# Loads, buffers and softmax steps of the first batch in an attention and two-layer MLP kernel

## The chip, the cores and the metric

The kernel runs on one core of a Trainium2 chip. The metric is the device time of one execution in microseconds (us), taken as the median over repeated runs.

## The reference

Inputs are float32 arrays; the host only rearranges them. Cut to what matters, with `S` = 576 positions, 4 batches, 8 heads of 64:

```python
scores = 0.125 * q @ k.T                              # per batch and head
# heads 0-3 see the last 32 positions, heads 4-7 every fourth of the last 128
scores = np.where(mask, scores, -1e9)
attn = np.exp(scores - scores.max(-1, keepdims=True))
attn = attn / (attn.sum(-1, keepdims=True) + 1e-9)
x = heads_side_by_side(attn @ v)                      # 2304 tokens x 512
x = ((x @ w1) * (x @ w2)) @ w3 @ w_out                # 512 -> 1024 -> 1024 -> 512
g = x @ w_gate
return (g / (1 + np.exp(-g)) * (x @ w_val)) @ w_out2  # 512 -> 1536 -> 512
```

## The kernel before

**Data.** The weights arrive as 8-byte floats in blocks of 1 MB (128 partitions x 2048 words of 32 bits). A block goes into one of four raw buffers (`raw0`, `raw1` and the two halves of `early`) and is converted there by five steps: ScalarE takes up the high words (`conv` piece 0), VectorE shifts the low words (piece 1) and joins both (piece 2), ScalarE rounds to the high part (piece 3), and VectorE subtracts to get the low part (piece 4). Piece 4 writes the weight slot and frees the raw buffer. A product of two float32 matrices is then three matmuls, high by high, high by low and low by high (`mm3`, lines 193 to 195). Every operand, attention's results too, is split into such parts by one ScalarE copy and one VectorE subtraction.

**Work.** Attention runs over 16 pairs of heads, four pairs for each batch. For a pair, TensorE makes the scores of all nine 64-row blocks (line 290), VectorE scales them and adds the mask (`masked`, line 301), takes the row maxima (`maxima`, line 313), ScalarE makes one exponential for each block column, with the row sum beside it (`exps`, line 318), VectorE inverts the sums (`inverse`, lines 323 and 324), and VectorE (first batch) or GpSimd (the others) multiplies (`normed`, line 329). A pair's nine columns are handled in two halves, of four (`g` = 0) and five columns (`g` = 1). Then come three groups of transposes (line 337), their copies (line 341), the products with v (line 355), and `attended`, which splits the result into the parts of x (lines 579 and 582).

The five chunks of tokens go through gates: `gate` k multiplies x by block k of w1 and of w2 (12 matmuls of 512 columns each), multiplies both and splits the product into `p`. `w_steps` multiply w3 by w_out, 512 columns of w3 in part 0 and 512 in part 1, and give the blocks `W`; `contraction` multiplies p by W. The first four gates of chunk 0 stand among the w_steps, since both need only weights, x and one another's buffers.

**Order.** Everything up to chunk 2 is a list of nodes. A node names its engine, an assumed duration, what it comes after and a key; `run_nodes` plays the list through with these assumptions (DMA at `DMA_RATE` MB per us behind one queue) and writes each engine's instructions in the order of that play. On the chip every engine keeps this order and waits by semaphores. So an instruction whose input is late holds up all that stand behind it on its engine. All loads are issued by SyncE (SP) in one such order, and one that has to wait for a buffer holds up those behind. `FIRST`, `EACH`, `START` and `W_AT` are times, in the same play, from which keys are made: the first pair, the distance of the pairs, the first gate and the first two w_steps. Later chunks and the second MLP are written out by hand in program order.

**Before the change** the start of the program loads k and q of pair 0, a mask, the first two weight blocks in four halves, and then k and q of pair 1, and so on; the first two w_steps stand among the attention of pairs 0 to 2. `v` and the scores buffers `s` are two each, used in turn.

Of the kernel before, what the change touches and what calls it, by code (L numbers as in the profile page):

```python
# [24 lines left out]
P = 128  # L25
# [65 lines left out]
FIRST, EACH, START = 4, 6, 36.0  # L91
W_AT = [10, 14]


def moe_chain_kernel(tc, q_in, k_in, v_in, w_in, mask_in, out):
# [8 lines left out]
    with static as st, other as ot, psum as pp, dram as dp:  # L104
# [9 lines left out]
        pr = fp.tile([P, 2, 2, CMAX], F32R, name="p")  # L114
# [99 lines left out]
        def gate_b(name, x, n):  # L214
            project(bb[:, :n], name, x)
            count["p"] += 1
            u, p = ta[:, :n], pr[:, count["p"] % 2, :, :n]
# [28 lines left out]
        att1_pool = tc.tile_pool(name="att1", bufs=1)  # L246
        att2_pool = tc.tile_pool(name="att2", bufs=1, side="right")
        with att1_pool as a1, att2_pool as a2:


            qd = [a1.tile([P, S], F32, name=f"q{i}") for i in range(2)]
            ks = [a1.tile([P, WIN + S], F32, name=f"k{i}") for i in range(2)]
            vv = [a1.tile([P, NBLK, P], F32, name="v0")]
            raw_pool = tc.tile_pool(name="rawx", bufs=1)
            rp = raw_pool.__enter__()
            pr_more = rp.tile([P, 2, 2, CMAX], F32R, name="p2")
            vv.append(rp.tile([P, NBLK, P], F32, name="v1"))
# [7 lines left out]
            sm = [a2.tile([P, 3, NBLK], F32, name=f"sm{i}") for i in range(2)]  # L265
# [7 lines left out]
            def v_of(i):  # L273
                return vv[i % 2 if i < NPAIR else 0]
# [21 lines left out]
            def masked(i, s_mm):  # L296
                s = sc[i % 2]
# [13 lines left out]
            def maxima(i, g):  # L311
                lo, hi = COLS[g]
                nc.vector.tensor_reduce(out=sm[i % 2][:, 0, lo:hi], in_=sc[i % 2][:, lo:hi], op=ALU.max, axis=AX.X, negate=True)  # L313

            def exps(i, g):
                s, m = sc[i % 2], sm[i % 2]
                for n in range(*COLS[g]):
                    nc.scalar.activation(s[:, n], s[:, n], AF.Exp, bias=m[:, 0, n:n + 1], accum_out=m[:, 1, n:n + 1])  # L318

            def inverse(i, g):  # L320
                lo, hi = COLS[g]
                m = sm[i % 2]
# [3 lines left out]
            def normed(i, g):  # L326
                s, m = sc[i % 2], sm[i % 2]
                lo, hi = COLS[g]
                (nc.vector if i < NPAIR else nc.gpsimd).tensor_tensor(
# [4 lines left out]
            def transposes(i, g, got):  # L334
                s = sc[i % 2]
# [319 lines left out]
            def v_loads(i, key=INF, after=()):  # L655
                loads["v", i] = node("SP", 0.47, load_v, i, after=[v_use.get(i - 2 if i <= NPAIR else i - 1), *after], mb=0.44, key=key)

            def attention(i, t, dt, after=()):

                b, hp = divmod(i, NPAIR)  # L660
                s_mm = node("PE", 1.05, scores, i, after=[loads["q", i], *s_use.get(i - 2, []), *after], key=t, take=("bank", 2))
                q_use[i] = s_mm
                m1 = node("DVE", 2 * on_dve(384) + 2 * on_dve(96), masked, i, s_mm, after=[s_mm, *s_use.get(i - 2, [])], give=[(s_mm, None)])
                e, x = [], []
                for g, (lo, hi) in enumerate(COLS):
                    r = node("DVE", on_dve(96 * (hi - lo)), maxima, i, g, after=[m1])
                    ex = node("ACT", (hi - lo) * 0.36, exps, i, g, after=[r])
                    nm = node("DVE", 0.28, inverse, i, g, after=[ex])
                    if i < NPAIR:
# [8 lines left out]
                s_use[i] = ts  # L678
# [3 lines left out]
                for g, cols in enumerate((half_of(i), S - half_of(i))):  # L682
# [4 lines left out]
                    outs.append(node("DVE", on_dve(cols) + 0.1, attended, i, g, 1, v_mm, after=[h, *beyond_use], give=[(v_mm, [g])]))  # L687
# [16 lines left out]
            def p_tile(c, k):  # L704
                return (pr_more[:, k - 2] if c == 0 and 2 <= k < 4 else pr[:, k % 2])[:, :, :CHUNKS[c][1]]

            def gate(c, k, key, dt=2.9):
# [7 lines left out]
                p = p_tile(c, k)  # L715
                buf = k if c == 0 and k < 4 else k % 2
                h, lo = parts(n, ta[:, :n], p[:, 0], p[:, 1], [bo, p_use.get(buf)])
# [35 lines left out]

            def open_stages():
                raw_pool.__exit__(None, None, None)
# [87 lines left out]
            stage_pool = tc.tile_pool(name="stages", bufs=1)  # L843
# [451 lines left out]
```

## Time and profile before

| | |
|---|---|
| median of 3 runs | 842.8 us (841.18, 842.8, 843.55) |
| the profiled execution, its own time | 842.12 us, of which the span of its instructions 839.9 us |
| TensorE (PE) busy | 810.7 us, 97% of the span |
| VectorE (DVE) / ScalarE (ACT) / GpSimd (POOL) busy | 545.5 / 428.8 / 97.0 us |
| mean granted TensorE clock | 0.98 of full speed |
| moved by DMA | 204.18 MB, 243 GB/s over the span |

All times in the rows are from the start of the span. PEld is the loading of stationary operands, which overlaps PE. A row of the timeline gives start, duration, engine, line, operation, tiles and count, and in brackets how long the engine had been idle before it and what ended that. Matmuls overlap, so a row's duration is longer than the distance to the next one. The granted clock has two levels here, 0.5 (1.2 GHz) and 1.0 (2.4 GHz); a value between them is a mean over a stretch.

### The profile page before, as it was taken

The page shows a single profiled execution, that of the slowest core. Times are in us where ns is not written, and L with a number is a line of the kernel's source. Part 1 is how long each engine was busy: PE and PEld are TensorE (multiplying, and loading weights), DVE is VectorE, ACT ScalarE, POOL GpSimd, SP SyncE. Part 2 cuts the span into 40 slices and gives each one's busy share as a digit, 9 for nine tenths or more (in the row PEclk, how much of TensorE's full clock was granted, in tenths as well). Part 3 has the DMA queues.
Part 4 walks back from the last instruction along what each step waited for, and adds up shares of the span by engine and source line. Part 5 has one row for each costly group of instructions (what it writes and reads, how often), then busy time and mean ns, then how long its engine had stood idle before and what let it go on. Part 6 is the DMA issues. An engine that isn't in the chain of part 4 may idle for free.

```text
span 839.9 us, 13927 instructions
## 1 busy us (share of the span) xinstructions
PE 810.7 (97%) x5242; PEld 734.9 (88%) x5242; DVE 545.5 (65%) x976; ACT 428.8 (51%) x1011; POOL 97.0 (12%) x128
## 2 busy tenths in 40 slices
PE   5689999999998999999999999999999999999998
PEld 3578887877786878788899999999999999999997
DVE  5889669486565733475676737587645677564867
ACT  4868387565665643344355634364444354353532
POOL 0000013654554521000000000000000000000000
PEclk7879999999998999999999999999999999999999
DMA  9988254979768850376699877788977787987735
GB/s 263 320 279 291 82 172 160 315 256 314 243 222 300 247 195 22 126 229 229 220 301 392 281 241 265 251 310 268 313 260 257 240 267 249 306 278 239 251 97 175
DMA packets 80530, 204.18 MB, mean 243 GB/s; under 512 B 5840, under 2 KB 41808, under 8 KB 75856
## 3 DMA queue, kind: packets, MB, share of 16 engines
q1 hardware_dynamic: 78736, 200.68, 71.9%
q10 hardware_dynamic: 1728, 2.62, 0.9%
q8 instruction: 41, 0.67, 0.3%
q14 instruction: 25, 0.20, 0.1%
HBM read 160.81 MB, written 42.47 MB: 242 GB/s over the span
## 4 chain that ended last, share of the span: by engine, by line
PE 75%; DMA 9%; DVE 8%; ACT 6%; issue 1%; SPq 1%; POOL 0%; ACTq 0%; DVEq 0%; POOLq 0%
PE bk L193 24%; PE bk L195 23%; PE bk L194 23%; DMA raw<-w_in 7%; ACT s L318 2%; PE bk L355 2%; PE bk L337 1%; DVE raw L820 1%; DVE raw L185 1%; DMA q<-q_in 1%; DVE s L301 1%; ACT raw L181 1%; PE bk L290 1%; ACT stage L831 1%; DVE sm L313 1%
## 5 line engine op out<-in xcount | busy, mean ns | idle before, releaser
L193 PE MATMUL bk<-x,w 128*128 128x512 f32 (+2 forms) x400 | 148.8, 373 | 1.0 <-ACT ta L212 1.0
L195 PE MATMUL bk<-x,w 128*128 128x512 f32 (+2 forms) x400 | 145.8, 365 | 0.0
L194 PE MATMUL bk<-x,w 128*128 128x512 f32 (+2 forms) x400 | 145.8, 364 | 0.0
L193 PEld LDWEIGHTS bk<-x,w 128*128 128x128 f32 x400 | 76.1, 190 | 12.5 <-ACT ta L212 1.6
L195 PEld LDWEIGHTS bk<-x,w 128*128 128x128 f32 x400 | 76.0, 190 | 10.7
L1162 DVE TENSOR_TENSOR acc<-bk,acc 128x384 f32<-128x384 f32 x102 | 56.0, 554 | 44.7 <-PE bk L195 44.5
L194 PEld LDWEIGHTS bk<-x,w 128*128 128x128 f32 x400 | 76.3, 191 | 9.5
L195 PE MATMUL bk<-po,wo 128*128 128x384 f32 x240 | 80.5, 335 | 0.0
L194 PE MATMUL bk<-po,wo 128*128 128x384 f32 x240 | 80.2, 335 | 0.0
L193 PE MATMUL bk<-po,wo 128*128 128x384 f32 x240 | 79.4, 336 | 0.3 <-DVE acc L1162 0.3
L833 POOL TENSOR_TENSOR stage<-raw,stage 128x256 fp32r<-128x256 f32 x96 | 71.4, 777 | 32.3 <-ACT stage L831 32.2
L193 PE MATMUL bk<-w 128*128 128x384 f32 (+1 forms) x216 | 73.1, 341 | 0.0
L194 PE MATMUL bk<-w 128*128 128x384 f32 (+1 forms) x216 | 73.1, 338 | 0.0
L195 PE MATMUL bk<-w 128*128 128x384 f32 (+1 forms) x216 | 72.5, 339 | 0.0
L1087 ACT ACTIVATE u<-bk 128x384 f32<-128x384 f32 x80 | 38.7, 489 | 53.4 <-PE bk L195 53.4
L160 ACT ACTIVATE po<-u 128x768 fp32r<-128x768 f32 (+1 forms) x64 | 50.9, 803 | 26.3 <-PE bk L195 10.5
L161 DVE TENSOR_TENSOR po<-u,po 128x768 fp32r<-128x768 f32 (+1 forms) x64 | 57.4, 902 | 8.7 <-ACT po L160 8.6
L318 ACT ACTIVATE s<-s,sm 128x96 f32<-128x96 f32 x144 | 51.8, 362 | 20.9 <-DVE sm L313 20.9
L195 PE MATMUL bk<-p,W 128*128 128x512 f32 (+1 forms) x160 | 58.3, 369 | 0.0
L194 PE MATMUL bk<-p,W 128*128 128x512 f32 (+1 forms) x160 | 58.2, 368 | 0.0
L193 PE MATMUL bk<-p,W 128*128 128x512 f32 (+1 forms) x160 | 57.7, 380 | 0.0
L181 ACT ACTIVATE raw<-raw 128x1024 f32<-128x1024 f32 (+1 forms) x32 | 34.9, 1090 | 30.0 <-DMA raw<-w_in 30.0
(145 smaller groups left out, 1728.2 us busy)
## 6 DMA issues: line engine op xcount, KB each, us to landing
w<-wd SPq DMA_DIRECT2D x70, 512.0 KB, 4.7
wo<-wod SPq DMA_DIRECT2D x63, 512.0 KB, 4.8
raw<-w_in SPq DMA_DIRECT2D x28, 1024.0 KB, 7.6
mid<-wd SPq DMA_DIRECT2D x42, 512.0 KB, 4.8
wd<-stage SPq DMA_DIRECT2D x16, 896.0 KB, 5.1
early<-w_in SPq DMA_DIRECT2D x8, 1024.0 KB, 7.3
wod<-stage SPq DMA_DIRECT2D x8, 896.0 KB, 6.3
wd<-u SPq DMA_DIRECT2D x8, 896.0 KB, 5.2
```

The lines of the kernel that those rows point to most:

```text
L160: nc.scalar.activation(hi, src, AF.Copy)
L161: return nc.vector.tensor_tensor(out=lo, in0=src, in1=hi.bitcast(F32), op=ALU.subtract)
L181: nc.scalar.activation(hi.bitcast(F32), hi.bitcast(F32), AF.Prelu, scale=REBIAS, alpha=SIGN_UP)
L185: nc.vector.scalar_tensor_tensor(out=lo, in0=hi, scalar=3, in1=lo, op0=ALU.logical_shift_left, op1=ALU.bitwise_or)
L193: nc.tensor.matmul(ps, wh, xh, start=start, stop=False, skip_group_check=onto)
L194: nc.tensor.matmul(ps, wh, xl, start=False, stop=False, skip_group_check=onto)
L195: nc.tensor.matmul(ps, wl, xh, start=False, stop=stop, skip_group_check=onto)
L318: nc.scalar.activation(s[:, n], s[:, n], AF.Exp, bias=m[:, 0, n:n + 1], accum_out=m[:, 1, n:n + 1])
L355: nc.tensor.matmul(banks_of[got[w]][j * D:(j + 1) * D, lo - w * half:hi - w * half], v_of(i)[:KW, n, j * D:(j + 1) * D], pt[:KW, c, z * QB ...
L833: nc.gpsimd.tensor_tensor(out=dst[:, :, 1], in0=src, in1=dst[:, :, 0].bitcast(F32), op=ALU.subtract)
L1087: nc.scalar.activation(t, src, AF.Copy)
L1162: nc.vector.tensor_tensor(out=a, in0=ps, in1=a, op=ALU.add)
```

## The change

The loads of the first batch's q, k, v and masks are keyed in front of all weight blocks, and all weight blocks wait in the plan until the scores of pair 0 are issued. Pairs 0 to 3 get a `v`, an `s` and an `sm` buffer each; these lie in a pool `front`, and the buffers of p, which used to be there from the start, are opened in its place when batch 0 is through with it. Half `g` = 1 of each pair of batch 0 no longer takes five exponentials: GpSimd adds the negated row maxima to the whole half (`shifted`), ScalarE takes one exponential of 480 columns (`exp_all`), and VectorE sums the rows (`sums_of`). The other half keeps its four exponentials. The VectorE node of `attended` gets a key instead of none, for all batches, and the mask is waited for by `masked` instead of by the scores. `parts` inside a gate is written as two nodes (`p_part`), since the p buffers exist only later.

```diff
-FIRST, EACH, START = 4, 6, 36.0
-W_AT = [10, 14]
+FIRST, EACH, START = 4, 5, 36.0
+W_AT = [24, 27]
+WIDE = [(i, 1) for i in range(4)]
+NORMV = [(i, j) for i in range(4) for j in range(2)]
...
-            vv = [a1.tile([P, NBLK, P], F32, name="v0")]
...
+            vv = [a2.tile([P, NBLK, P], F32, name="v0")]
+            front_pool = tc.tile_pool(name="front", bufs=1)
+            fr = front_pool.__enter__()
+            vv += [fr.tile([P, NBLK, P], F32, name=f"v{i}") for i in range(1, NPAIR)]
...
+            sm = [a2.tile([P, 3, NBLK], F32, name=f"sm{i}") for i in range(4)]
+            sc += [fr.tile([P, NBLK, KW], F32, name=f"s{i}") for i in range(2, NPAIR)]
...
+            def shifted(i, g):
+                s, m = sc[sc_of(i)], sm[sc_of(i)]
+                lo, hi = COLS[g]
+                nc.gpsimd.tensor_tensor(
+                    out=s[:, lo:hi], in0=s[:, lo:hi],
+                    in1=m[:, 0, lo:hi].unsqueeze(2).to_broadcast([P, hi - lo, KW]), op=ALU.add,
+                )
+
+            def exp_all(i, g):
+                lo, hi = COLS[g]
+                nc.scalar.activation(sc[sc_of(i)][:, lo:hi], sc[sc_of(i)][:, lo:hi], AF.Exp)
+
+            def sums_of(i, g):
+                lo, hi = COLS[g]
+                nc.vector.tensor_reduce(out=sm[sc_of(i)][:, 1, lo:hi], in_=sc[sc_of(i)][:, lo:hi], op=ALU.add, axis=AX.X)
...
-                    ex = node("ACT", (hi - lo) * 0.36, exps, i, g, after=[r])
+                    if in_one(i, g):
+                        ex = node("POOL", (0.79, 0.95)[g], shifted, i, g, after=[r])
+                        ex = node("ACT", on_act(96 * (hi - lo)), exp_all, i, g, after=[ex])
+                        ex = node("DVE", on_dve(96 * (hi - lo)), sums_of, i, g, after=[ex])
+                    else:
+                        ex = node("ACT", (hi - lo) * 0.36, exps, i, g, after=[r])
...
-                    outs.append(node("DVE", on_dve(cols) + 0.1, attended, i, g, 1, v_mm, after=[h, *beyond_use], give=[(v_mm, [g])]))
+                    outs.append(node("DVE", on_dve(cols) + 0.1, attended, i, g, 1, v_mm, after=[h, *beyond_use], key=t + dt + 5, give=[(v_mm, [g])]))
...
             q_loads(0, 0)
-            mask_at = [node("SP", 0.47, load_mask, slice(0, NHALF), mb=0.2, key=0.1)]
-            for n in range(2):
-                conversion(n, 0.2 + 0.1 * n)
-            q_loads(1, 1)
-            v_loads(0, 2)
-            attention(0, FIRST, 6, mask_at)
...
+            mask_at = [node("SP", 0.47, load_mask, slice(0, NHALF), mb=0.2, key=-9)]
+            q_loads(1, 0.2)
+            v_loads(0, 6)
+            for i in range(NPAIR):
                 if i >= 2:
...
+                    q_loads(i, 0.6)
+                if i == 2:
+                    mask_at.append(node("SP", 0.47, load_mask, slice(NHALF, NHALF + NBLK), after=[q_use[0]], mb=0.44, key=5))
+                if i:
+                    v_loads(i, 6 + i, [q_use[0]])
+                attention(i, FIRST + EACH * i, 6, mask=mask_at[i // 2])
+            for n in range(12):
                 conversion(n, after=[q_use[0]])
...
+            opened = node("SP", 0.0, open_p, after=[*v_use.values(), *[t for ts in s_use.values() for t in ts]])
+            for i in range(NPAIR):
+                p_use[i] = opened
```

**The queue of loads, at the start of the program.** SyncE's rows before; `k0` and `q0` are the buffers of the even pairs, `k1` and `q1` those of the odd ones, and `raw0`, `raw1`, `early` take weights:

```order
L271 DMA k0_101<-k_in 128x576
L268 DMA q0_99<-q_in 128x576
L560 DMA mask_113<-mask_in 128x384
L570 DMA raw0_78<-w_in 128x1024 x2
L570 DMA raw1_79<-w_in 128x1024 x2
L271 DMA k1_102<-k_in 128x576
L268 DMA q1_100<-q_in 128x576
L277 DMA v0_103<-v_in 96x1152
L271 DMA k0_101<-k_in 128x576
L268 DMA q0_99<-q_in 128x576
L560 DMA mask_113<-mask_in 128x864
L277 DMA v1_108<-v_in 96x1152
```

And after the change, from the fifth load on (ahead of these stand a mask, k0, q0 and k1):

```order
L273 DMA q1_96<-q_in 128x576
L282 DMA v0_99<-v_in 96x1152
L276 DMA k0_97<-k_in 128x576
L273 DMA q0_95<-q_in 128x576
L587 DMA mask_110<-mask_in 128x864
L282 DMA v1_103<-v_in 96x1152
L282 DMA v2_104<-v_in 96x1152
L276 DMA k1_98<-k_in 128x576
L273 DMA q1_96<-q_in 128x576
L282 DMA v3_105<-v_in 96x1152
L597 DMA raw0_77<-w_in 128x1024
L597 DMA raw1_78<-w_in 128x1024
```

The first weights stood fourth in the queue; now they stand fifteenth, behind everything that batch 0's attention reads.

**ScalarE at the start of the program.** Before: `raw0`, `raw1` are raw weights, `s0` the scores of pair 0 and `sm0` its maxima and sums, `W2` and `w` weight slots:

```order
L181 ACTIVATE raw0_78<-raw0_78 128x512 x2
L318 ACTIVATE s0_110,sm0_115<-s0_110,sm0_115 128x96 x5
L181 ACTIVATE raw1_79<-raw1_79 128x512
L318 ACTIVATE s0_110,sm0_115<-s0_110,sm0_115 128x96 x4
L174 ACTIVATE W2_74<-raw0_78 128x512
L174 ACTIVATE w_66<-raw1_79 128x512
L181 ACTIVATE raw1_79<-raw1_79 128x512
```

After, with `s1` the scores of pair 1, and `pt` the copies of transposes:

```order
L323 ACTIVATE s0_107,sm0_112<-s0_107,sm0_112 128x96 x4
L341 ACTIVATE s0_107<-s0_107 128x480
L323 ACTIVATE s1_108,sm1_113<-s1_108,sm1_113 128x96 x4
L368 ACTIVATE pt_109<-bk4_85 96x384
L341 ACTIVATE s1_108<-s1_108 128x480
L368 ACTIVATE pt_109<-bk5_86 96x384
```

Five exponentials of 96 columns became one of 480, and no weight stands between the pairs.

**VectorE where pair 12, the first pair of batch 3, is masked.** Before: `raw1` is a weight block of the second MLP, `x0` the parts of x that pair 11's results go to, `s0` with `mask` pair 12:

```order
L582 TENSOR_TENSOR x0_76<-bk7_89,x0_76 128x2x96
L391 COPY beyond_109<-bk7_89 128x2x48
L582 TENSOR_TENSOR x0_76<-bk6_88,x0_76 128x2x96
L391 COPY beyond_109<-bk6_88 128x2x48
L582 TENSOR_TENSOR x1_838<-beyond_109,x1_838 128x2x192 x2
L183 TENSOR_SCALAR raw1_79<-raw1_79 128x1024
L301 SCALAR_TENSOR_TENSOR s0_110<-bk7_89,mask_113 128x384
L301 SCALAR_TENSOR_TENSOR s0_110<-bk7_89,mask_113 64x96
L301 SCALAR_TENSOR_TENSOR s0_110<-bk6_88,mask_113 128x384
L301 SCALAR_TENSOR_TENSOR s0_110<-bk6_88,mask_113 64x96
```

After:

```order
L185 TENSOR_SCALAR raw1_78<-raw1_78 128x1024
L187 SCALAR_TENSOR_TENSOR raw1_78<-raw1_78 128x1024
L609 TENSOR_TENSOR x0_76<-bk7_88,x0_76 128x2x96
L418 COPY beyond_106<-bk7_88 128x2x48
L609 TENSOR_TENSOR x0_76<-bk6_87,x0_76 128x2x96
L418 COPY beyond_106<-bk6_87 128x2x48
L786 COPY o1_80<-bk1_82 128x512
L865 TENSOR_TENSOR raw1_78<-raw1_78 128x256
L609 TENSOR_TENSOR x1_924<-beyond_106,x1_924 128x2x192 x2
L865 TENSOR_TENSOR raw1_78<-raw1_78 128x256 x3
L306 SCALAR_TENSOR_TENSOR s0_107<-bk7_88,mask_110 128x384
L306 SCALAR_TENSOR_TENSOR s0_107<-bk7_88,mask_110 64x96
```

The first VectorE step of the same weight block, which stood right ahead of the masking, now stands ahead of pair 11's results. On TensorE the distance from this pair's scores to its transposes grows from 36 matmuls of 512 columns to 39 and the scores of pair 13.

## Rows read from the trace of the kernel before

**Rows 1.** Windows: busy time by engine, PEclk, DMA share, GB/s.
```profile
0.00:50.60 50.60, 31.25 (x370) 23.06 (x370) 37.26 (x82) 33.40 (x106) 0.82 (x8) 0.75 0.97 294
50.60:78.80 28.20, 28.20 (x123) 23.29 (x122) 26.57 (x32) 21.68 (x24) 0.00 (x0) 0.97 0.79 272
78.80:261.90 183.10, 181.85 (x1361) 145.89 (x1359) 126.52 (x239) 114.63 (x337) 69.83 (x88) 1.00 0.69 232
261.90:264.90 3.00, 0.04 (x1) 0.00 (x0) 2.93 (x8) 2.46 (x10) 1.88 (x3) 0.85 0.90 363
264.90:270.70 5.80, 5.79 (x15) 4.50 (x16) 0.51 (x1) 2.50 (x8) 5.45 (x8) 0.50 0.38 128
270.70:839.90 569.20, 563.54 (x3378) 538.20 (x3376) 351.74 (x617) 254.13 (x530) 19.05 (x22) 1.00 0.72 241
```
**Rows 2.** Timeline of PE: last attention of batch 0, first gate.
```profile
45.53 1.27 PE L337 MATMUL bk<-ident,s 128*96 128x128 f32 x5 [1.34 <-ACT x L579]
48.28 2.40 PE L355 MATMUL bk<-pt,v 96*64 96x64 f32 x40 [1.48 <-ACT pt L341]
50.62 0.80 PE L193 MATMUL bk<-x,w 128*128 128x512 f32 x1
```
**Rows 3.** Timeline of DVE and POOL around pair 12.
```profile
249.68 1.72 DVE L582 TENSOR_TENSOR x<-beyond,x 128x384 fp32r<-128x384 f32 x2
255.52 0.70 DVE L183 TENSOR_SCALAR raw<-raw 128x1024 uint32<-128x1024 uint32 x1 [4.12 <-DMA raw<-w_in]
256.13 1.44 DVE L301 SCALAR_TENSOR_TENSOR s<-bk,mask 128x384 f32<-128x384 f32 x4
...
264.00 0.85 POOL L329 TENSOR_TENSOR s<-s,sm 128x384 f32<-128x384 f32 x1 [0.72 <-DVE sm L324]
```
**Rows 4.** Timeline of PE there: pair 12's scores, a full-clock matmul, the transposes.
```profile
252.50 1.04 PE L290 MATMUL bk<-k,q 64*64 64x96 f32 x36
...
261.55 0.39 PE L195 MATMUL bk<-x,w 128*128 128x512 f32 x1
264.91 0.88 PE L337 MATMUL bk<-ident,s 128*96 128x128 f32 x3 [2.97 <-POOL s L329]
```
**Rows 5.** Issues of loads by SP, and the DMA view's landing of two of them.
```profile
2.12 1.85 SPq L570 DMA_DIRECT2D raw<-w_in  x4
11.12 0.33 SPq L277 DMA_DIRECT2D v<-v_in  x1
38.88 0.33 SPq L570 DMA_DIRECT2D early<-w_in  x1
...
v<-v_in SPq DMA_DIRECT2D x1, 432.0 KB, 11.8
early<-w_in SPq DMA_DIRECT2D x1, 1024.0 KB, 10.2
```
**Rows 6.** Groups of DVE by form, 0 to 100 us: count, busy us, mean ns.
```profile
L185 DVE SCALAR_TENSOR_TENSOR early<-early 128x1024 uint32<-128x1024 uint32 x8 | 9.8, 1222 | 0.2
L183 DVE TENSOR_SCALAR raw<-raw 128x1024 uint32<-128x1024 uint32 x8 | 5.5, 686 | 0.0
L176 DVE TENSOR_TENSOR w<-raw,w 128x1024 fp32r<-128x1024 f32 x4 | 4.9, 1222 | 0.0
L301 DVE SCALAR_TENSOR_TENSOR s<-bk,mask 128x384 f32<-128x384 f32 x8 | 4.4, 548 | 7.3 <-PE bk L290 7.3
L329 DVE TENSOR_TENSOR s<-s,sm 128x480 f32<-128x480 f32 x4 | 2.6, 657 | 0.1
L313 DVE TENSOR_REDUCE sm<-s 128x5 f32<-128x480 f32 x4 | 2.6, 646 | 0.0
```
**Rows 7.** Timeline of DVE: first masking, one block's steps, the last block of part 0.
```profile
7.21 1.45 DVE L301 SCALAR_TENSOR_TENSOR s<-bk,mask 128x384 f32<-128x384 f32 x4 [5.82 <-PE bk L290]
...
60.47 1.23 DVE L176 TENSOR_TENSOR w<-early,w 128x1024 fp32r<-128x1024 f32 x1
61.61 1.22 DVE L185 SCALAR_TENSOR_TENSOR raw<-raw 128x1024 uint32<-128x1024 uint32 x1
62.75 0.69 DVE L582 TENSOR_TENSOR p<-ta,p 128x512 fp32r<-128x512 f32 x1
75.25 1.22 DVE L176 TENSOR_TENSOR W<-early,W 128x1024 fp32r<-128x1024 f32 x1
```
**Rows 8.** Windows for DVE's busy time (third pair of numbers).
```profile
7.20:50.60 43.40, 25.54 (x320) 20.52 (x320) 36.77 (x81) 32.12 (x105) 0.00 (x0) 0.71 1.01 304
0.00:76.50 76.50, 57.15 (x480) 44.46 (x481) 61.53 (x112) 53.56 (x129) 0.82 (x8) 0.82 0.91 288
```
**Rows 9.** Groups: a small exponential on ACT, a multiplication on POOL.
```profile
L318 ACT ACTIVATE s<-s,sm 128x96 f32<-128x96 f32 x36 | 12.9, 361 | 0.5 <-DVE sm L313 0.5
L329 POOL TENSOR_TENSOR s<-s,sm 128x480 f32<-128x480 f32 x12 | 11.9, 993 | 189.8 <-DVE sm L324 167.2 <-ACT s L318 22.6
```
**Rows 10.** Timeline: a VectorE subtraction beside work of POOL.
```profile
202.66 0.86 POOL L329 TENSOR_TENSOR s<-s,sm 128x384 f32<-128x384 f32 x1 [0.72 <-DVE sm L324]
...
202.74 1.32 DVE L582 TENSOR_TENSOR p<-ta,p 128x512 fp32r<-128x512 f32 x1
```

More of the change, by code (lines that the diff above doesn't have):

```diff
@@ L264, in moe_chain_kernel, with sc_of @@
             ident = a2.tile([P, P], F32, name="ident")
-            sm = [a2.tile([P, 3, NBLK], F32, name=f"sm{i}") for i in range(2)]
+            sm = [a2.tile([P, 3, NBLK], F32, name=f"sm{i}") for i in range(4)]
+            sc += [fr.tile([P, NBLK, KW], F32, name=f"s{i}") for i in range(2, NPAIR)]
+            def sc_of(i):
+                return i if i < NPAIR else i % 2
             def load_q(i):
@@ L655, in v_loads, with attention @@
             def v_loads(i, key=INF, after=()):
-                loads["v", i] = node("SP", 0.47, load_v, i, after=[v_use.get(i - 2 if i <= NPAIR else i - 1), *after], mb=0.44, key=key)
-            def attention(i, t, dt, after=()):
+                loads["v", i] = node("SP", 0.47, load_v, i, after=[v_use.get(0 if i == NPAIR else i - 1) if i >= NPAIR else None, *after], mb=0.44, key=key)
+            def attention(i, t, dt, after=(), mask=None):
                 b, hp = divmod(i, NPAIR)
-                s_mm = node("PE", 1.05, scores, i, after=[loads["q", i], *s_use.get(i - 2, []), *after], key=t, take=("bank", 2))
+                s_mm = node("PE", 1.05, scores, i, after=[loads["q", i], *s_use.get(sc_of(i), []), *after], key=t, take=("bank", 2))
                 q_use[i] = s_mm
-                m1 = node("DVE", 2 * on_dve(384) + 2 * on_dve(96), masked, i, s_mm, after=[s_mm, *s_use.get(i - 2, [])], give=[(s_mm, None)])
+                m1 = node("DVE", 2 * on_dve(384) + 2 * on_dve(96), masked, i, s_mm, after=[s_mm, mask, *s_use.get(sc_of(i), [])], give=[(s_mm, None)])
                 e, x = [], []
@@ L704, in p_tile, with p_part @@
             def p_tile(c, k):
-                return (pr_more[:, k - 2] if c == 0 and 2 <= k < 4 else pr[:, k % 2])[:, :, :CHUNKS[c][1]]
+                return p_bufs[k if c == 0 and k < 4 else k % 2][:, :, :CHUNKS[c][1]]
+            def p_part(c, k, piece):
+                u, p = ta[:, :CHUNKS[c][1]], p_tile(c, k)
+                if piece == 0:
+                    act_copy(p[:, 0], u)
+                else:
+                    dve_rest(p[:, 1], u, p[:, 0])
             def gate(c, k, key, dt=2.9):
@@ L714, in gate @@
                 bo = node("DVE", on_dve(n), gate_out, c, "w2", after=[b, ao])
-                p = p_tile(c, k)
                 buf = k if c == 0 and k < 4 else k % 2
-                h, lo = parts(n, ta[:, :n], p[:, 0], p[:, 1], [bo, p_use.get(buf)])
+                h = node("ACT", on_act(n), p_part, c, k, 0, after=[bo, p_use.get(buf)])
+                lo = node("DVE", on_dve(n), p_part, c, k, 1, after=[h])
                 p_of[c, k] = lo, buf
@@ L751, in stored, with open_p @@
                 nc.sync.dma_start(out=x2d[m, :, first:first + n], in_=ost[got_of(d)[0]][:, :n])
+            def open_p():
+                front_pool.__exit__(None, None, None)
+                for pool, n in ((p_pool, 0), (more_pool, 2)):
+                    pp = pool.__enter__()
+                    p_bufs.extend(pp.tile([P, 2, CMAX], F32R, name=f"p{n + i}") for i in range(2))
             def open_stages():
-                raw_pool.__exit__(None, None, None)
+                more_pool.__exit__(None, None, None)
                 sp = stage_pool.__enter__()
```

49 lines of the change are left out of this document (21 added, 28 removed).

## The prediction

> **What bounds the kernel now.** I read the windows first [rows 1]. From 50.6 us to the end TensorE is busy for all but a few us: nothing is missing up to 78.8, 1.25 us in the next 183, and 5.7 in the last 569. So the time is the moment at which the first gate starts, plus a fixed amount of matmuls, plus the holes behind it. There are two places worth money. The first is the front: 31.25 of 50.6 us busy, and much of that at half clock (0.75 on average). The timeline there [rows 2] shows TensorE waiting for ScalarE's copies and ending batch 0's last product at 50.6, from where the gates run without a break. The second is one hole: 2.97 us without a matmul up to 264.9, and after it 5.8 us at a granted clock of 0.50, which at full clock would have been 2.9. Together that is 2.97 + 2.9 = 5.9 us. Its cause stands in the timeline of VectorE [rows 3, 4]: pair 12's scores end at 253.5, but masking starts at 256.13, since the shift of a weight block stands ahead of it and waited 4.12 us for that block to land; GpSimd's second multiplication then ends at 264.85, and the transposes start right there.
>
> In the front it is VectorE that paces, with DMA beside it. From its first masking at 7.2 to 50.6 it is busy 36.8 of 43.4 us [rows 7, 8], and the DMA share is 1.01 in that stretch [rows 8].
>
> **The front, what VectorE must do before the first gate.** The gate needs pair 3's results and the third weight block (the first of w1 and w2). By the new order this stands ahead of it on VectorE, priced by its groups [rows 6], where a following instruction starts about 0.08 earlier than the duration says [rows 7]: four maskings at 1.45 (5.8), eight maxima (4.1 with 0.57 and 0.46), eight inverses of some 0.4 (3.2), eight multiplications (0.58 and 0.47, 4.2), the four pairs' results (about 0.85 twice and 1.27 twice, 4.2), the four half blocks of weights (1.55 each, 6.2), the third block and the two first steps of the fourth (2 x 0.61 + 3 x 1.14 = 4.6), and new: four row sums, not in the trace. They read 480 columns and give five, as the maxima do, so I take 0.57 each, 2.3; the nearest other row is the multiplication's 0.58, so both ends are the same to me. That is 34.6 us. It begins at 7.2 as before: k and q of pair 0 are now second and third behind a small mask, and the warm-up matmuls held the scores until then anyway. Without a wait the work would end at 41.8; with the 6.6 us of idle time that VectorE has now in this stretch, at 48.4. I take 4.2 us of waits, since pairs still wait for each other, and get **46.0** against 50.62, a gain of 4.6 (2.2 to 8.8).
>
> What the other edits do there: the five exponentials that go took five starts of 0.36, 1.8 us of ScalarE [rows 9]; the one of 480 columns I put between that row's 0.36 and the 1.8, at 0.6. It comes after an addition on GpSimd, not seen with an addition so far, but its multiplication of the same shape takes 0.99 [rows 9]. So the half is no faster by itself (1.0 + 0.6 against 1.8), and ScalarE is freed by 1.2 us a pair. ScalarE was idle 34% of the front [rows 1], so I price this at nothing; where ScalarE is late, up to 4.8 us over four pairs lie within the 6.6 of waits already taken. The own buffers for `v` and `s` let the loads run ahead; the mask moved from the scores to the masking, the p buffers opened later (ready well before the first p, which comes two projections after pair 3 is done) and the two nodes for one cost nothing, for the same reason.
>
> GpSimd's additions could slow VectorE. The row: a subtraction on VectorE took 1.32 us beside a multiplication on GpSimd [rows 10], where the same form took 0.69 alone [rows 7], so 0.63 is lost. Four additions would be at most 2.5 us; in the new order they stand beside maxima and maskings, which read one or no operand of the same kind, so I take nothing and keep 2.5 for the range. The Trainium skill (SBUF — State Buffer, section "SBUF: two separate sides") states that VectorE instructions with two SBUF inputs and GpSimd instructions lock the shared port pair for a whole instruction, the other one waiting; by that, four additions of 0.99 could cost 4.0 us and the first gate would start at 50.0, next to no gain. The row with its 0.63 speaks for less than a whole instruction of 0.86.
>
> **Do the weights keep up?** They come later now: 15 loads stand ahead of them instead of three. What follows on TensorE from the first gate to the last w_steps of part 0 took 28.2 us, 123 matmuls [rows 1]. In the new order the fourth gate's first projection (12 matmuls, 2.75) and two pairs' scores (1.04 each [rows 4]) stand in this stretch too: 33.0, so these w_steps are due at 46.0 + 33.0 = 79.0. Because 4.8 us of other work are then already done, the gain stays 4.6 there, and it would be zero if they started at 83.6.
> They need block 12 of the weights. Up to it the new queue moves 19.6 MB (7 pairs' k and q at 0.59, 5 v at 0.44, masks 0.64, 12 blocks at 1.05). Before, 13.3 MB (6 pairs, 4 v, masks, 7 blocks) had landed at 38.88 + 10.2 = 49.1 [rows 5]; in proportion, 19.6 land at 72.4. Two other rates: v of pair 1 landed at 11.12 + 11.8 = 22.9 with 5.4 MB [rows 5], which gives 83; the 304 GB/s of the front [rows 8] give 64.5. From landing to its last step VectorE has 6.6 us by the new order (this block's 0.61, 1.14 and 1.22, the block before's 1.14, the next one's 0.61, and gate and softmax steps of 1.9), so the block is ready at **79.0**, between 71 and 90. By VectorE's work alone: it had done 61.5 us when the same block was ready at 76.5 [rows 7, 8]; it now has 2.3 for sums and 3.3 for pair 4 more, and 1.1 of a later block less, 66.0, and with 6.7 idle ahead of the first masking and 4.2 of waits that is 76.9. So supply and need meet within a us or two. I take no stall, and keep 83 + 6.6 for the range.
>
> **The hole before pair 12.** The key on `attended` and the shifted start give another order there. The late shift now stands ahead of pair 11's results, and 39 matmuls and another pair's scores, 9.9 us, lie between pair 12's scores and its transposes, where there were 36 (8.2). From the start of masking to GpSimd's end took 8.7 us [rows 3]; started at the end of the scores, that fits into 9.9. So the hole and its half clock go: **minus 5.9**. What is late next: the shift may still wait, then it holds pair 11's results, for which the gates of the next chunk wait. Against that, GpSimd's parts of the block ahead, on which the load of this one waits, now stand before pair 11's multiplications and not behind them, so I expect the load earlier. If it waits as before, the hole stays at another place for the same 5.9.
> Seven pairs (7 to 11, 14, 15) now have only 36 matmuls between scores and transposes; six had (8, 11 to 15). 8.2 us are just short of 8.7, and one more weight step of 1.22 stands ahead of pair 8's masking, so I add 2 us of small waits there (0 to 5.9).
>
> **Sum.** The profiled execution took 842.12, of which 839.9 span; 842.1 - 4.6 - 5.9 + 2 = 833.6. The median of the runs is 0.7 above this execution, so about **834**.
>
> **Rivals.**
> 1. The hole only moves: front better, but one wait of a pair or of a weight costs 5.9 as now: 842.8 - 4.6 + 2 = 840. For it speaks that waits for loads are not known to the order, and the seven tight pairs.
> 2. The front gives nothing, since the weights are late just so much (ready at 83.6): 842.8 - 5.9 + 2 = 839. For it speaks the DMA share of 1.01.
> 3. Slower: the same mechanism further. With the rate that v of pair 1 saw, block 12 is ready at 90, 6.4 us later than 83.6, and a hole of this size is longer than the one that cost half the clock, so another 2.9: 842.8 + 6.4 + 2.9 - 5.9 + 2 = 848. It decides from about 86 on. Against it: the weights' larger transfers moved faster than v's.
> 4. The change does nothing that is seen: neither gain, 842 to 844. The blank front speaks against it.
>
> **How the numbers follow.** I give my forecast (830 to 837) 0.50, rival 1 0.27, rival 2 0.10, rival 3 0.08, rival 4 0.05. A measurement of this kernel tells apart about 0.3%, 2.5 us. Faster than 840.3 are the forecast, two thirds of rival 1 and most of rival 2: 0.75. Same: the rest of these and rival 4, 0.16. Slower: rival 3, 0.09. The range goes from 828 (first gate at 42, no small waits) to 843 (rivals 1, 2 and 4).
>
> **What would show it.** Right: no weight load issued before pair 3's v; the first gate between 44 and 48; VectorE without long idle time from 7 to 80; the last w_steps of part 0 near 79 without a wait for VectorE; no TensorE idle of 2 us between 100 and 330, and no stretch at half clock there. Wrong: the first gate past 50, TensorE waiting for VectorE's weights between 50 and 90 at a lowered clock, VectorE waiting for `raw` with a masking or results behind it, or GpSimd's additions with VectorE rows stretched beside them.

## The result, and the profile after

The changed kernel took 834.46 us (median of 4 runs, 832.68 to 835.79) against 842.17 for the kernel before on the same chip; the ratio is 0.9906 with a 95% interval of 0.9882 to 0.993. A second comparison gave 835.39 us and 0.9924 (0.9905 to 0.9944). The forecast was 834. The profiled execution took 835.79 us, the slowest of its four, with a span of 834.0.

The rows below are of the same kinds as those of before: first TensorE's timeline, every stop of 0.9 us or more from the first gate to pair 14.

```profile
44.38 0.39 PE L195 MATMUL bk<-x,w 128*128 128x512 f32 x1
...
45.93 0.50 PE L197 MATMUL bk<-x,w 128*128 128x512 f32 x1 [0.94 <-DVE w L178]
...
85.81 0.50 PE L195 MATMUL bk<-W,w 128*128 128x512 f32 x1 [1.58 <-DVE W L609]
...
178.44 0.53 PE L364 MATMUL bk<-ident,s 128*96 128x128 f32 x3 [1.91 <-POOL s L356]
...
240.69 0.86 PE L364 MATMUL bk<-ident,s 128*96 128x128 f32 x6 [1.90 <-POOL s L356]
...
290.19 1.04 PE L295 MATMUL bk<-k,q 64*64 64x96 f32 x36 [1.27 <-DVE beyond L418]
```

The first gate starts at 44.38 instead of 50.62 [rows 2], and stops after two matmuls for VectorE's last step of the third block. The windows of the changed kernel (columns as in [rows 1]) show VectorE busy 33.90 of 38.80 us, and the clock already full from 40 us on, where before it stood at 0.50 until the first gate was under way (second fence, the kernel before in the same stretch):

```profile
7.20:46.00 38.80, 26.83 (x360) 21.49 (x359) 33.90 (x84) 25.47 (x69) 4.20 (x4) 0.78 0.89 289
34.00:40.00 6.00, 5.51 (x21) 4.14 (x20) 6.00 (x14) 4.18 (x8) 0.00 (x0) 0.70 0.66 142
40.00:46.00 6.00, 4.87 (x55) 3.87 (x55) 4.70 (x8) 4.48 (x7) 0.00 (x0) 1.00 0.79 328
240.00:280.00 40.00, 39.31 (x308) 31.93 (x309) 28.27 (x56) 27.02 (x83) 22.66 (x29) 1.00 0.78 267
```
```profile
40.00:46.00 6.00, 3.90 (x47) 3.34 (x48) 5.93 (x13) 5.49 (x18) 0.00 (x0) 0.50 0.99 299
46.00:52.00 6.00, 4.52 (x47) 3.75 (x46) 4.18 (x8) 3.50 (x7) 0.00 (x0) 0.50 0.94 311
52.00:58.00 6.00, 6.00 (x27) 4.91 (x26) 5.37 (x9) 4.63 (x5) 0.00 (x0) 0.97 0.63 218
```

The hole of [rows 3, 4] is gone, and 240 to 280 has the full clock throughout. VectorE's timeline there (changed kernel) shows pair 12's masking directly behind its scores, and the late shift behind it:

```profile
254.71 1.46 DVE L306 SCALAR_TENSOR_TENSOR s<-bk,mask 128x384 f32<-128x384 f32 x4 [1.19 <-PE bk L295]
256.19 1.11 DVE L318 TENSOR_REDUCE sm<-s 128x5 f32<-128x480 f32 x2
257.96 1.34 DVE L185 TENSOR_SCALAR raw<-raw 128x1024 uint32<-128x1024 uint32 x1 [0.65 <-DMA raw<-w_in]
```

Where the time went is read at points that all kernels here share: pair 8's scores, ahead of which each has issued the same TensorE work (1159 matmuls), and a wait near 410 us for `ta`, the buffer of a gate's product, from which the program is the same text. Pair 8's scores start at 167.09 (before 170.30), the stop for `ta` ends at 406.03 (413.23), the span ends at 834.0 (839.9). So the front gives 3.2, the stretch of batches 2 and 3 gives 4.0, and 1.3 us were lost behind that in this execution. The medians differ by 7.7, in the second comparison by 5.9.

### The profile page after: what moved, and what is told of

It reads as the page before. It is cut to its first block, busy times and chain, and to the rows that moved or that the text cites. A ratio compares the mean times of both kernels' runs of the same rounds, so it can differ in the third digit from the quotient of the medians.

```text
span 834.0 us, 13900 instructions
## 1 busy us (share of the span) xinstructions
PE 807.8 (97%) x5242; PEld 732.4 (88%) x5242; DVE 545.0 (65%) x980; ACT 423.6 (51%) x975; POOL 101.5 (12%) x132
## 4 chain that ended last, share of the span: by engine, by line
PE 75%; DVE 11%; DMA 7%; ACT 3%; issue 2%; POOL 1%; SPq 0%; ACTq 0%; POOLq 0%; DVEq 0%
PE bk L195 24%; PE bk L197 23%; PE bk L196 23%; DMA raw<-w_in 6%; PE bk L382 2%; DVE raw L187 2%; PE bk L364 1%; DVE w L178 1%; PE bk L295 1%; DVE s L306 1%; DMA x2d<-o 1%; POOL stage L878 1%; DVE sm L318 1%; DVE early L187 1%; ACT s L323 1%
## 5 line engine op out<-in xcount | busy, mean ns | idle before, releaser
L195 PEld LDWEIGHTS bk<-x,w 128*128 128x128 f32 x400 | 75.3, 188 | 12.3 <-ACT ta L214 0.9
L197 PEld LDWEIGHTS bk<-x,w 128*128 128x128 f32 x400 | 75.3, 188 | 11.7 <-DVE w L178 1.4
L196 PEld LDWEIGHTS bk<-x,w 128*128 128x128 f32 x400 | 75.4, 188 | 9.5
L323 ACT ACTIVATE s<-s,sm 128x96 f32<-128x96 f32 x124 | 44.7, 363 | 26.3 <-DVE sm L318 26.3
L1148 ACT ACTIVATE g<-g 128x384 f32<-128x384 f32 x54 | 28.1, 521 | 40.2 <-DVE g L1143 40.1
```

The source lines that it names most:

```text
L195: nc.tensor.matmul(ps, wh, xh, start=start, stop=False, skip_group_check=onto)
L196: nc.tensor.matmul(ps, wh, xl, start=False, stop=False, skip_group_check=onto)
L197: nc.tensor.matmul(ps, wl, xh, start=False, stop=stop, skip_group_check=onto)
L1148: nc.scalar.activation(dst, src, AF.Silu)
```

## The experiments

All times are medians of 4 to 12 runs; the ratio is to the kernel before in the same job.

**The changed kernel again.** No edit.

> The changed kernel once more, to see how firm its holes are from one execution to the next. If the waits behind the first gate (1.58 us at 85.8, 1.9 each ahead of the transposes of pairs 8 and 11, 1.3 at 290) come from the order of the instructions, they stand in this execution too, within some tenths, and the time is 834.5, between 833 and 836. If they come from loads that happen to be late, one or two of them are gone or elsewhere and the time can differ by 2 to 3 us.

835.39 us. The stops are there again with 1.57, 1.50, 1.88 and 0.85 us for 1.58, 1.91, 1.90 and 1.27, so they belong to the order. The first gate came at 43.33 here, against 44.38: in one and the same order it moves by a microsecond.

**Parts of the change undone, one at a time.** First the key on `attended` left out, for all batches.

```diff
-outs.append(node("DVE", on_dve(cols) + 0.1, attended, i, g, 1, v_mm, after=[h, *beyond_use], key=t + dt + 5, give=[(v_mm, [g])]))
+outs.append(node("DVE", on_dve(cols) + 0.1, attended, i, g, 1, v_mm, after=[h, *beyond_use], give=[(v_mm, [g])]))
```

> The changed kernel without the key on VectorE's part of attended. Theory (the front and the hole before pair 12 are two gains of their own): the first gate still starts at 44 to 46, so the front's 6 us stay; behind it pairs 10, 13 and 14 now have 9 to 12.5 us between scores and transposes, the others 8.2; holes of one or two us each, and the time is 834 to 838. First rival (the key brings the gain): a hole of 3 us with half clock comes back somewhere between 150 and 300, and the time is 838 to 842. Second rival (the key costs as much as it gives): 832 to 834.

839.01 us, ratio 0.9962 (0.9946 to 0.9977). The first rival's time came, and its hole of 3 us; what neither it nor the theory had is that the loss begins in the front, where pair 8's scores start at 171.50, 4.4 later than with the key. TensorE's timeline of this run, and the window behind the hole:

```profile
48.82 0.79 PE L195 MATMUL bk<-x,w 128*128 128x512 f32 x1 [2.10 <-DVE beyond L418]
...
264.89 0.53 PE L364 MATMUL bk<-ident,s 128*96 128x128 f32 x3 [3.14 <-POOL s L356]
```
```profile
264.90:270.90 6.00, 6.00 (x31) 5.07 (x32) 2.99 (x4) 5.52 (x14) 6.00 (x8) 1.00 0.39 131
```

Without the key pair 3's products stand behind all the first w_steps, and VectorE takes up its results at 47.41; the gate waits. The hole came back with the full clock behind it, not half, so the 2.9 us that half clock cost there in the kernel before are not a fixed part of its price.

Then the old exponentials in both halves.

```diff
-WIDE = [(i, 1) for i in range(4)]
+WIDE = []
```

> The changed kernel with the old exponentials in both halves, so without the additions on GpSimd and the four row sums on VectorE. Theory (VectorE paces the front): the four row sums of 0.57 us are gone there, so the first gate starts up to 2.3 us earlier, near 42 to 43.5, and the time is 832 to 834. Rival (the chain of a pair paces it, five exponentials of 0.36 against addition, one exponential and a sum): the first gate starts no earlier, or up to 2 us later, and the time is 834 to 837.

832.13 us, ratio 0.9883 (0.9864 to 0.9902), faster than the changed kernel, whose interval in the same job does not meet this one. The theory's time came, its reason did not: the first gate starts later, at 46.58, since TensorE waits for longer in the pairs (5.24 us ahead of pair 0's transposes, 2.97 for pair 2's copies), and pair 8's scores come at 166.96, as before the edit. A later gate costs nothing here, because the waits of 0.94, 0.41, 1.58 and 0.27 us behind it have become one of 1.31 at 80.87.

Two buffers in turn (`sc_of`; `v_of` and `v_loads` likewise).

```diff
-                return i if i < NPAIR else i % 2
+                return i % 2
```

> The changed kernel with two v, s and sm buffers used in turn, as before, the new keys of the loads kept. By the order two weight halves now stand ahead of the last k, q and v, pair 2's scores stand behind pair 0's transposes and pair 3's behind pair 1's. Theory (the buffers are what lets the pairs overlap): VectorE waits for pairs, first gate at 46 to 49, and since the weights are then late by as much or less, the time is 835 to 839. Rival (VectorE's work paces the front, the buffers give nothing): first gate at 44 to 45, time 833 to 836.

837.18 us, ratio 0.9935 (0.9917 to 0.9954), in the theory's range for the time; the gate came later than it had (50.30 for 46 to 49). The buffers are worth 2 us or so: TensorE waits 6.73 us for pair 0 and 4.22 for pair 2 in turn.

The front's loads, keys and distances as before.

```diff
-FIRST, EACH, START = 4, 5, 36.0
-W_AT = [24, 27]
+FIRST, EACH, START = 4, 6, 36.0
+W_AT = [10, 14]
...
+            for n in range(2):
+                conversion(n, 0.2 + 0.1 * n)
-            q_loads(1, 0.2)
-            v_loads(0, 6)
+            q_loads(1, 1)
+            v_loads(0, 2)
...
```

> The changed kernel with the loads, keys and distances of the front as before (weights fourth in the queue, W_AT 10 and 14, EACH 6); own buffers, one exponential per half, the key on attended and the later p buffers stay. Theory (the order of the loads makes the front's gain: q and k of pair 1 stand behind 2 MB of weights again): pair 1's scores come near 15 us, VectorE waits there, first gate at 48 to 50, time 838 to 841. Rival (buffers and softmax make it): first gate at 45 to 47, time 833 to 836.

844.22 us, ratio 1.0031 (1.002 to 1.0042): slower than the kernel before. The theory named the place, but not the size. TensorE's timeline:

```profile
16.30 1.87 PE L295 MATMUL bk<-k,q 64*64 64x96 f32 x36 [8.00 <-DMA q<-q_in]
...
53.75 0.79 PE L195 MATMUL bk<-x,w 128*128 128x512 f32 x1 [2.09 <-DVE beyond L418]
```

So without the new loads, with their keys and distances, nothing of the front's gain is left; which of these three carries it was not tried apart. Own buffers, one exponential per half and the key, put on the old front, lose 2.3 us, and the stop of 2.1 us ahead of the gate is the one that the key alone brings to the old front (next run).

**Parts of the change alone.** The key in the kernel before (the same line as in `no_key`, the other way round).

> The kernel before with the key on attended alone. Theory: the hole of 2.97 us before pair 12 and its half clock go (minus 5.9), the pairs with 8.2 us between scores and transposes give back some 4 as in the changed kernel, and the first gate stays at 50.6: 838 to 841. First rival (the hole only went because the front moved): it stays, 842 or more. Second rival (the key alone carries the change): 834 to 836.

841.76 us, ratio 1.0003 (0.999 to 1.0016): nothing, so the theory's time did not come. Yet the hole went, as it said. What the key takes away in the front shows in the windows of this run, to be set beside 0.97 for 52 to 58 us in the kernel before:

```profile
51.10 0.79 PE L193 MATMUL bk<-x,w 128*128 128x512 f32 x1 [2.13 <-DVE beyond L391]
...
246.81 0.86 PE L337 MATMUL bk<-ident,s 128*96 128x128 f32 x6 [2.08 <-POOL s L329]
```
```profile
46.00:52.00 6.00, 3.31 (x42) 3.02 (x43) 5.66 (x9) 4.55 (x7) 0.00 (x0) 0.50 0.75 239
52.00:58.00 6.00, 6.00 (x17) 4.63 (x17) 2.09 (x3) 1.44 (x3) 0.00 (x0) 0.57 0.74 288
```

TensorE stops for 2.13 us right ahead of the first gate, and the gate then runs at half clock almost to 58. Pair 8's scores come at 174.06, 3.8 us later than before; the stop for `ta` at 411.75, 1.5 earlier. So in this profile the late part gained 5.2 and the front lost 3.8; the medians show no difference at all.

The key together with the later transposes of `room`, below, in the kernel before.

> The kernel before with the two things that act behind batch 0 only: the key on attended, and the transposes of pairs 8 to 15 planned 2.95 us later. Against room (830.8) it lacks the front alone. If the front is worth what the profiles show at pair 8's scores (3 to 4 us): 834 to 835. If it is worth what the first gate shows (6 to 7 us): 837 to 838. If nothing in the late part is gained without the front: 841 or more.

836.79 us, ratio 0.9951 (0.9932 to 0.9969). Against the next run (830.79, 0.9868) the front is worth 6 us, 7 by the ratios, nearer to what the gate shows. In the two profiles the whole difference stands in the front: pair 8's scores at 175.35 and 168.01, and from there to the stop for `ta` 234.6 and 234.9 us. The key fits this again: this old front has the stop (2.11 us ahead of the gate at 52.12) and the half clock behind it (0.56 from 52 to 58), so the two fronts differ by more than the profiles of before and after do.

**More room for a softmax.** The changed kernel with the transposes of pairs 8 to 15 planned later.

```diff
-attention(NPAIR * (c + 1) + i, a + T * (1 + 5 * i), 3 * T)
+attention(NPAIR * (c + 1) + i, a + T * (1 + 5 * i), 4 * T)
```

> The changed kernel with the transposes of pairs 8 to 15 planned 2.95 us later after their scores (4 T for 3 T); by the new order 12.0, 18.0, 8.9 and 11.7 us of matmuls lie between scores and transposes of pairs 8 to 11, where there were 8.2. Theory (8.2 us are just too short for a softmax of 8.7 with a weight step in its way): the two waits of 1.5 to 1.9 us ahead of the transposes of pairs 8 and 11 go, and the time is 831 to 833. Rival (late loads hold up whatever stands behind them, the distance does not matter): waits of the same sum stand elsewhere, before gates or scores, and the time is 834 to 836.

830.79 us, ratio 0.9868 (0.985 to 0.9887). The theory holds, at a time just under its 831: between 103 and 402 us only two stops of 0.2 us or more are left in TensorE's timeline.

```profile
184.66 0.50 PE L195 MATMUL bk<-p,W 128*128 128x512 f32 x1 [0.52 <-ACT o L784]
...
296.56 0.53 PE L364 MATMUL bk<-ident,s 128*96 128x128 f32 x3 [0.65 <-POOL s L356]
```

**What paces the front.** The changed kernel in the same order, each new row sum made three times, or replaced by a constant.

```diff
-                nc.vector.tensor_reduce(out=sm[sc_of(i)][:, 1, lo:hi], ...)
+                for _ in range(3): nc.vector.tensor_reduce(out=sm[sc_of(i)][:, 1, lo:hi], ...)
```
```diff
-                nc.vector.tensor_reduce(out=sm[sc_of(i)][:, 1, lo:hi], ...)
+                nc.vector.memset(sm[sc_of(i)][:, 1, lo:hi], 30.0)
```

> The changed kernel with each of the four new row sums made three times, in the same order: eight more VectorE instructions of 0.57 us, 4.6 us, all ahead of the first gate. Theory (VectorE paces the front and the weights meet TensorE without slack): the first gate starts 3.5 to 4.6 us later, near 48, the last w_steps of part 0 too, and the time is 838 to 840. Rival (the pairs' own waits or the loads pace it): VectorE's idle time of 4 to 5 us in the front takes them up, and the time is 834 to 836.

837.69 us, ratio 0.9954 (0.9936 to 0.9972). Between the two: the median is 2.3 to 3.2 us higher than the changed kernel's two (2.5 to 4.0 by the ratios), half or more of the added 4.6. The first gate starts at 46.59; with an unaltered front it came at 43.33, 44.38 and, in `room`, 45.26.

> The changed kernel in the same order, with a constant in place of the four row sums, so that the softmax of half a batch 0 pair is divided by a wrong number and each of these VectorE instructions is some 0.1 us instead of 0.57. Theory (VectorE paces): first gate 1 to 2 us earlier, time 832.5 to 834. Rival (supply of the weights, the loads, paces the last w_steps): the first gate comes earlier, but TensorE waits as much longer for the weights near 78 and 85, and the time is 834 to 836.

835.64 us, ratio 0.993 (0.9905 to 0.9956): no gain. The first gate starts at 45.00, so the theory fails here, and the rival too, since the waits at 79.61 and 86.47 are 0.39 and 1.57 as ever. Work that is added to VectorE arrives in good part, work that is taken away does not. Up to 46 us VectorE has 1.8 us less to do (32.06 for 33.90 busy) and waits for as much longer: 1.24 us for the second mask to land, where it had not waited, and 2.03 for ScalarE's part of pair 0's results for 1.48. So the third pair's products already start no earlier, at 31.69 against 31.32 (changed kernel, then this run):

```profile
31.32 2.40 PE L382 MATMUL bk<-pt,v 96*64 96x64 f32 x40 [2.03 <-ACT pt L368]
```
```profile
31.69 2.26 PE L382 MATMUL bk<-pt,v 96*64 96x64 f32 x40 [2.03 <-ACT pt L368]
```

Behind that TensorE is itself near the limit: from 34 to 40 it is busy 5.51 of 6.00 us at a clock of 0.70 (windows of after, above), with the first w_steps and pair 3. The clock's rise differs between executions, and the gate with it: 36 to 38 had 1.00 in the execution whose gate came at 43.33, and 0.50 in this one.

**Both, and one more.** Later transposes with the old exponentials; and with pairs 4 and 5 held back too (`last_step` is the last matmul node of part 0's w_steps).

```diff
-                attention(NPAIR + i, START + T * (12 + 5 * i), 3 * T, started_gates)
+                attention(NPAIR + i, START + T * (12 + 5 * i), 3 * T, [last_step])
```

> Both in one: old exponentials in both halves, and the transposes of pairs 8 to 15 planned 2.95 us later. If the 3 us of no_wide and what room gives are independent, 829 to 831; if no_wide's gain only comes from the later waits, no better than the better one of the two, 831 to 833.

829.61 us, ratio 0.9857 (0.9839 to 0.9875): the lowest median, 1.4% below the kernel before and some 5 us below the changed one. Against `room` it is 1.2 us, and those intervals overlap.

> The version of room_nowide with the scores of pairs 4 and 5 held back until the last w_steps of part 0, as they stood before the change. Theory (softmax of these pairs and its GpSimd multiplications, which slow VectorE from 1.22 to 2.0 us, stand in the way of the weights): no wait of 1.3 us near 80, and the time is 827 to 829. Rival (these pairs then have 7.9 us again between scores and transposes and wait there): 829.5 to 832.

830.06 us, ratio 0.9866 (0.9829 to 0.9902): no gain, and the rival's time. The wait near 80 is gone, and stops of 0.47, 0.22, 0.83 and 0.49 between 82 and 146 stand in its place; the 0.83 is one of those that the rival named, ahead of transposes.

## Why the prediction came true, step by step

**The sum.** The forecast of 834 was met to half a microsecond, and part of that is luck. Between the two profiles the change is worth 5.9 us, where the sum had 8.5: the front gave 3.2 for 4.6, the stretch with the hole 4.0 for 3.9, and 1.3 were lost where the sum had nothing. The changed kernel's median lies 1.3 below its profiled execution, which hides half of the difference; its second median, 835.39, is 5.9 us below the kernel before.

**The front's VectorE sum.** The prices hold. The groups of the changed kernel, up to 100 us:

```profile
L345 DVE TENSOR_REDUCE sm<-s 128x5 f32<-128x480 f32 x4 | 2.6, 645 | 0.0
...
L341 ACT ACTIVATE s<-s 128x480 f32<-128x480 f32 x4 | 2.4, 593 | 0.1
...
L334 POOL TENSOR_TENSOR s<-s,sm 128x480 f32<-128x480 f32 x4 | 4.2, 1049 | 21.4 <-DVE sm L318 19.8 <-DVE sm L350 1.6
```

0.645 us a sum (0.57 once the next one's early start is taken off), 0.59 for the exponential of 480 columns where 0.6 was taken, about 1.0 for the addition. The third block was ready at 45.9 against the forecast 46.0; the gate itself could start at 44.38, because its first two matmuls read only high parts. But the term rested on VectorE alone. `three_sums` shows that more work on VectorE there costs time; `no_sums` shows that less work on it would not have come through, since waits for a mask and for ScalarE take its place up to 32 us, and behind that TensorE does, at half clock for part of it. So VectorE paces the front together with these, not by itself.

**Additions on GpSimd at nothing.** Nearly right in the profile: three of the four took 0.99 us, the fourth 1.23, begun 0.16 behind a VectorE multiplication, and masking beside the first took 1.45 as without. What the step did not look at were the multiplications of pairs 4 and 5. They move from 107 us, where no weights are converted beside them (0.99 and 0.83 us there), into the conversion, and there both engines lose. VectorE, then GpSimd, changed kernel:

```profile
73.77 1.19 DVE L187 SCALAR_TENSOR_TENSOR early<-early 128x1024 uint32<-128x1024 uint32 x1
74.87 2.02 DVE L178 TENSOR_TENSOR w<-early,w 128x1024 fp32r<-128x1024 f32 x1
...
77.70 1.19 DVE L178 TENSOR_TENSOR W<-early,W 128x1024 fp32r<-128x1024 f32 x1
78.81 1.86 DVE L187 SCALAR_TENSOR_TENSOR raw<-raw 128x1024 uint32<-128x1024 uint32 x1
```
```profile
74.00 1.80 POOL L356 TENSOR_TENSOR s<-s,sm 128x480 f32<-128x480 f32 x1 [46.98 <-DVE sm L351]
77.93 1.65 POOL L356 TENSOR_TENSOR s<-s,sm 128x384 f32<-128x384 f32 x1 [2.12 <-DVE sm L351]
```

The subtraction takes 2.02 for 1.22 us, the multiplication 1.80 for 0.99: each loses 0.8. The order of the starts shows in the rows: the multiplication begins 0.23 behind VectorE's join (73.77) and ends 0.84 after it, then the subtraction ends 1.09 after the multiplication. The Trainium skill (SBUF — State Buffer, section "SBUF: two separate sides") lets one of the two engines wait for the whole instruction of the other; the trace agrees within 0.2 us, since 2.02 is close to 1.22 + 0.99. The prediction read its row of 0.63 as less than such a wait. That reading was wrong: in [rows 10] the multiplication began 0.08 earlier, so of its 0.86 us 0.78 were left when the subtraction began, and the 0.63 lost is that less 0.15, where the subtraction above ends 0.13 sooner than a full 1.22 behind the multiplication. Taking this collision away did not shorten the kernel (`pair45_late`).

**The weights meet TensorE.** The time is right to a tenth: block 12 was forecast for 79.0, its last step ends at 78.9 (the row at 77.70 above), and TensorE waited 0.41 us for it at 78.95. But two errors cancel in it. The forecast let the block land at 72.4, by what the queue had to move. SyncE issued its load at 63.42, as soon as VectorE's last step on an earlier block (62.17 to 63.39) had freed the buffer, and it landed 6.3 us later, near 69.7. VectorE, SyncE and the DMA view, changed kernel:

```profile
62.17 1.22 DVE L178 TENSOR_TENSOR w<-early,w 128x1024 fp32r<-128x1024 f32 x1
...
71.70 0.69 DVE L185 TENSOR_SCALAR early<-early 128x1024 uint32<-128x1024 uint32 x1
```
```profile
63.42 0.33 SPq L597 DMA_DIRECT2D early<-w_in  x1
```
```profile
early<-w_in SPq DMA_DIRECT2D x1, 1024.0 KB, 6.3
```

So the supply followed the buffers that VectorE frees, and not the number of loads ahead (of which 14 stand before the first weights, not 15). From there VectorE was busy without a break and took 9.2 us to the block's last step, where the forecast had 6.6: it counted one step of the block before, and there were two, the join at 70.57 and the stretched subtraction at 74.87. What "I take no stall" missed stands right behind: the 1.58 at 85.81, where the next w_steps need results of the last ones split by VectorE (L609), and these splits stand behind the subtraction of the next block. Together with 0.94 at the gate and 0.27 at 101 the waits between gate and pair 8 are 3.2 us. So of 6.2 us at the gate about 3.2 arrive at pair 8's scores, where 4.6 were forecast: this term was too large by 1.4.

**The hole before pair 12.** Right for the place, as `key_only` and the profile after show; of the 5.9 us the 2.9 at half clock belong to that execution, since `no_key` has the hole without them. That 8.2 us are just short of 8.7 came in two of the seven tight pairs only: pairs 8 and 11 wait 1.9 each, the other five not, and in both a load was late. In pair 8 a late shift (VectorE waits 1.14 us for `raw`), two result steps and another weight step stand ahead of masking; in pair 11 it is ScalarE, whose part of a late block stands ahead of the exponentials:

```profile
234.19 1.17 ACT L183 ACTIVATE raw<-raw 128x1024 f32<-128x1024 f32 x1 [2.82 <-DMA raw<-w_in]
235.26 0.36 ACT L323 ACTIVATE s<-s,sm 128x96 f32<-128x96 f32 x1
```

This is rival 1's mechanism at a smaller price. The term was 2 us for small waits; the row at 290 included, they are 5.1 against 2.3 before (without the hole). Hole and waits together gave 4.0 between pair 8 and the stop for `ta`, where the forecast had 3.9. That `room` takes 4 us off and leaves waits of 0.52 and 0.65 shows that the distance was the waits' cause. The rows explain 3.1 of the 4.0 (minus 5.9, plus 5.1, minus 2.3); the other 0.9 lies in TensorE's busy time at full clock in this stretch, and the rows don't tell why.

**The rivals.** Rival 1, the hole at another place, came in part, as those two waits of 1.9, without loss of clock in this profile; rival 2 in part, as the 3.2 us behind the gate. Rivals 3 and 4 did not come. Of what was to show it: SyncE issues the first weights right behind pair 3's v, the first gate came at 44.38 (43.33 in the second profile, just under the stated 44), and there is no stop of 2 us and no half clock from 100 to 330 (the second profile has a few us of it, shown at the end).

```profile
11.70 0.61 SPq L282 DMA_DIRECT2D v<-v_in  x1
12.35 4.54 SPq L597 DMA_DIRECT2D raw<-w_in  x4
```

**What the sum hid.** It treated front and hole as two terms that add up, with the key on `attended` in the second alone. Four medians taken together say otherwise: 841.24 for the kernel before, 841.76 with the key alone, 839.01 with everything but the key, 835.39 with both. In the old front the key costs as much as it gains behind; in the new front leaving it out costs 4 us. Both the key in the old front and its lack in the new one bring a stop of 2.1 us ahead of the first gate. The forecast took the key as a matter of pair 12 alone.

**Left open.** Why `no_wide` gains 3 us over the changed kernel: up to the stop for `ta` the profiles put it at less than 1, against the medians' 2.3 to 3.3; and with later transposes it is 1.2. That the one exponential per half is no gain is shown; its price is not. The mask that `masked` waits for and the p buffers opened later were not tried apart.

## What to carry to other kernels

An earlier start of the bottleneck engine is worth what is left of it at the next point where it needs something that did not move: look for these points (here the weights' last block and the splits behind it) before counting the gain. In a list where engines keep a fixed order, the distance between producer and consumer has to hold the whole chain between them plus one late load; giving 3 us more to eight pairs was worth 4 us. Try each edit of a bundle alone and left out: here one did nothing alone and 4 us in company, and one was better left out.

## What the runs showed of the hardware

The price of a stop of TensorE in clock is not told by its length. 2.97 us in the kernel before were followed by 5.8 us at 0.50 [rows 1], 3.14 us in `no_key` and 2.08 in `key_only` by none; 1.90 us in the changed kernel by none, and 1.88 at the same place in its second profile by a few us at half clock. These are the stretches behind the stops in `key_only`, in the changed kernel, and in its second profile:

```profile
246.80:252.80 6.00, 6.00 (x31) 5.07 (x32) 2.09 (x4) 4.68 (x12) 5.72 (x8) 1.00 0.48 179
```
```profile
240.70:244.00 3.30, 3.30 (x18) 2.84 (x19) 0.48 (x1) 2.64 (x8) 3.30 (x5) 1.00 0.38 159
```
```profile
239.00:245.00 6.00, 5.58 (x22) 4.54 (x23) 1.20 (x2) 3.10 (x10) 5.44 (x8) 0.72 0.53 202
```

A stop went with a larger loss ahead of the first gate. In `key_only` and `before_room`, where TensorE stopped for 2.1 us there with the clock still at 0.50, 52 to 58 us has 0.57 and 0.56; in the kernel before, without that stop, it has 0.97. That is some 2.4 us of full clock in 6, besides the stop itself.
